# Loading a part of the gate matrix through chosen DMA engines, early in the stream

## The chip, the cores and the metric

One NeuronCore of a Trainium2 chip runs the whole kernel. The metric is the device time of one execution in microseconds (us); the time of a kernel is the median of its runs. A profile is one further execution, recorded by the hardware profiler, and its span runs from the first to the last instruction.

## The reference

A decode step for four sequences (B = 4, one token each, D = 512) mixes an attention branch and a gated feed-forward branch, with a gate g for each sequence:

```python
W = min(4096, max(256, Sk // 4))                # Sk = 16384, so W = 4096
q = (x @ wq).reshape(B, 1, 32, 128)             # 32 query heads on 8 key/value heads
scores = q . k_cache[:, :, Sk-W:, :] * 128**-0.5
a = (softmax(scores) . v_cache[:, :, Sk-W:, :]) @ wo       # wo: 4096 x 512
gate = x @ W_gate; gate = gate * (gate > 0)     # W_gate, W_up: 512 x 1792
b = (gate * (x @ W_up)) @ W_down                # W_down: 1792 x 512
g = sigmoid((x * gate_w).sum(-1))
out = g * a + (1 - g) * b
```

All inputs are bf16. The windows of the K and V caches are 64 MB, the matrices wq and wo 4 MB each, the three feed-forward matrices 1.8 MB each: 81 MB are read once for a result of 4 KB.

## The kernel before

The cache is cut into 8 sets (4 heads of one sequence each, NSET = 8). K of a set and V of a set are 4 MB each, 32 KB on every one of the 128 partitions; they pass through four such slots (NSLOT = 4). For each set VectorE transposes K in four parts (EKT, line 491), TensorE multiplies it by the query (SC), VectorE adds a mask and takes a running maximum (ESC, 527), ScalarE makes the exponentials (EXP, 619), VectorE transposes these (EPT, 542) and TensorE multiplies by V (PV). At the end come the gate and up products (GU: 16 matmuls each, 448 columns wide, 4 for each quarter q of the 512 input rows), the product with W_down (FFN), the gathering of the heads (OQ), and the product with wo (WO).

All loads are issued by SyncE's sequencer (SP), in the order of `_dma_order`: wq, x, gate_w, k 0, k 1, v 0, then k and v in turn, W_gate (`wg`), W_up, v 7, W_down, and wo in five pieces. A load into a slot waits until the one that used the slot before is done with it (`_slots`). Every engine executes its own list in order; a wait names an event that another engine or a load counts up.

A load of 128 partitions is spread over the core's 16 DMA engines, 8 partitions each. W_gate is laid out with four rows on each partition: partition p holds the rows 4p to 4p + 3 (`(p t) f -> p (t f)`), and quarter q of GU uses the rows 4p + q. x is turned to match: four small transposes (XT, line 324) take every fourth element of x, VectorE copies them to xT (EXT, 495), and ScalarE makes from the last column the gate's weights (GWB, 600).

The last piece of wo, 256 columns of 128 partitions, is not one load but three (`wo_rows`, from LOW3): of 123, 3 and 2 partitions. The page's line L256 is `load`, which issues every transfer; L320 and L324 are the helpers that issue matmuls and transposes, and L296 the one for GpSimd's masks. GpSimd (POOL) makes constants at the start, until 12.05 us, and does nothing after.

Of the kernel before, what the change touches and what calls it, by code (L numbers as in the profile page):

```python
# [5 lines left out]
FP32 = mybir.dt.float32  # L6
# [10 lines left out]
FF = 1792  # L17
# [7 lines left out]
OUTT = 2  # L25
OW = 512 // OUTT
OR = 128 // OUTT
WO_PIECES = ((0, 34), (34, 52), (52, 60), (60, 63), (63, 64))
LOW3 = (0, 123, 126, 128)

class _Plan:

# [70 lines left out]
def _alloc(nc, ctx):  # L103
    R = {}

    def sb(name, shape, dt):
        R[name] = ctx.enter_context(nc.sbuf_tensor(name, shape, dt))

    sb("slots", [128, NSLOT, 16384], BF16)
    sb("kt", [128, 4, 4096], BF16)  # L110
    sb("sc", [128, 2048], BF16)
    sb("pe", [128, 2048], BF16)
    sb("pT", [128, 2, 2048], BF16)
    sb("qblk", [128, NSET, 2, 144, 2], BF16)
    sb("xsb", [5, 512], BF16)
    sb("xT", [128, 20], BF16)
    sb("osb", [128, NSET, 512], BF16)
    sb("oq", [128, 32, 4], BF16)
    sb("identb", [128, 128], BF16)
    sb("identf", [128, 128], FP32)  # L120
    sb("ones", [128, 128], FP32)
    sb("ee", [16, 128], BF16)
    sb("e4", [16, 128], BF16)
    sb("rfold", [128, 128], FP32)
    sb("grpb", [128, 128], BF16)
    sb("own8", [128, 8], FP32)
    sb("scl", [128, 8], FP32)
    sb("maskl", [128, 128], BF16)
    sb("maskr", [128, 512], BF16)
    sb("maskf", [128, 512], BF16)  # L130
    sb("gwB", [128, 4, 128], BF16)
    sb("fold", [128, 4, 4, 64], BF16)
    sb("mx4", [128, 4], FP32)
    sb("rd32", [128, 8, 4], BF16)
    sb("negmax", [128, 2], FP32)
    sb("rowsum", [128, NSET], FP32)
    sb("recip", [128, 4, 4], FP32)
    sb("ge", [128, 2, 4], FP32)
    sb("gp", [128, 2, 4], FP32)
    sb("gg", [128, 2, 4], FP32)  # L140
    sb("hg", [128, 14, 4], BF16)
    sb("osum", [4, 512], BF16)
    R["psum"] = ctx.enter_context(nc.psum_tensor("bank", [128, 8, 512], FP32))
    return R

# [11 lines left out]


def _dma_order():
    o = [("wq",), ("x",), ("gw",), ("k", 0), ("k", 1), ("v", 0)]  # L160
    for s in range(2, NSET):
        o += [("k", s), ("v", s - 1)]
    return o + [("wg",), ("wu",), ("v", NSET - 1), ("wd",)] + [("wo", p) for p in range(len(WO_PIECES))]


def _slots():

    frees = [[] for _ in range(NSLOT)]
    at, wait = {}, {}
    turn = 0  # L170
    for it in _dma_order():
        k = it[0]
        if k in ("x", "gw") or (k == "wo" and it[1] > 0):
            continue
        if k == "wu":
            at[it] = at[("wg",)]
            wait[it] = wait[("wg",)]
            continue
        n = turn % NSLOT
        turn += 1  # L180
        at[it] = n
        wait[it] = list(frees[n])
        frees[n] = {"k": [("E", "KT", it[-1], 3)], "v": [("PV", it[-1])], "wq": [("Q", 1)], "wg": [("GU", 1)], "wd": [], "wo": []}[k]
    return at, wait


def _program(nc, plan, R, aps):
# [5 lines left out]
    xsb, xT, osb, oq = R["xsb"], R["xT"], R["osb"], R["oq"]  # L193
    identb, identf, ones = R["identb"], R["identf"], R["ones"]
    mx4, rd32, negmax, rowsum, recip = R["mx4"], R["rd32"], R["negmax"], R["rowsum"], R["recip"]
    ge, gp, gg, osum = R["ge"], R["gp"], R["gg"], R["osum"]
    consts = {"mask": R["maskf"], "grp": R["grpb"], "rfold": R["rfold"]}

    at, slot_wait = _slots()
# [39 lines left out]
        n = scf[key] - NSC  # L239
        return [("E",) + sck[n]] if n >= 0 else [("INIT",)]  # L240

    def wo_rows(p):

        return [slice(a, b) for a, b in zip(LOW3, LOW3[1:])] if p == len(WO_PIECES) - 1 else [slice(0, 128)]

    def set_of(s):
        return s % 4, s // 4
# [4 lines left out]
    def sync(e):  # L252
        E = _Eng(plan, e, "sp")

        def load(ev, ctr, dst, src, waits=()):
            E.op(lambda: e.dma_start(dst, src), ev=ev, waits=waits, ctr=ctr)  # L256

        for it in _dma_order():
            k = it[0]
            w = slot_wait.get(it, [])  # L260
            if k == "x":
                load(("X",), "d_x", xsb[0:4, :], A_x.rearrange("b o d -> (b o) d"))
            elif k == "gw":
                load(("GW",), "d_gw", xsb[4:5, :], gate_w.rearrange("(o p) -> o p", o=1))
            elif k == "wq":
                load(("WQ",), "d_wq", slot("wq"), A_wq.rearrange("(p t) f -> p (t f)", t=4), waits=w)
            elif k == "wg":
                load(("WG",), "d_wg", Wg, B_W_gate.rearrange("(p t) f -> p (t f)", t=4), waits=w)
            elif k == "wu":
                load(("WU",), "d_wu", Wu, B_W_up.rearrange("(p t) f -> p (t f)", t=4), waits=w)  # L270
            elif k == "wd":
                load(("WD",), "d_wd", Wd, B_W_down.rearrange("(p i) c -> p (i c)", i=14),
                     waits=w)
            elif k == "wo":
                lo, hi = WO_PIECES[it[1]]
                wo = A_wo.rearrange("(p i) c -> p (i c)", i=32)
                for n, r in enumerate(wo_rows(it[1])):
                    load(("WO", it[1], n), f"d_wo{it[1]}", Wo[r, OW * lo:OW * hi], wo[r, OW * lo:OW * hi], waits=w)
            else:
                b, qq = set_of(it[1])  # L280
                src = (A_k_cache if k == "k" else A_v_cache)[b, 4 * qq:4 * qq + 4, SK - WIN:SK, :]
                load((k.upper(), it[1]), f"d_{k}{it[1] % 3}", slot(*it), src.rearrange("h (r c) d -> r h (c d)", r=32),
                     waits=w)
        load(("OUT",), "d_out", out.rearrange("b o d -> (b o) d"), osum[:, :], waits=[("OSUM", 1), ("OSUM", 0)])
        E.wait([("OUT",)])

    def gpsimd(e):
# [24 lines left out]
        for g in range(8):  # L312
            v = R["fold"][:, g % 4, :, :]
            aff(v, v, [[1, 4], [-1, 64]], -64 * g, ne, 1.0, ("FOLD", g), mult=4)

    def tensor(t):
        E = _Eng(plan, t, "pe")

# [4 lines left out]
        def tp(out_, in_, idn, ev=None, waits=()):  # L323
            E.op(lambda: t.transpose(out_, in_, idn), ev=ev, waits=waits)  # L324
# [8 lines left out]
        def XT():  # L333
            bk = bankb[tr(("XT",))]
            for q in range(4):
                tp(bk[:, 6 * q:6 * q + 5], xsb[0:5, q:q + 509:4], identb[0:5, 0:5], ev=("XT",) if q == 3 else None,
                   waits=tr_free(("XT",)) + [("X",), ("GW",), ("IDB",)])

        def Z():
            for q in range(4):  # L340
# [65 lines left out]
        def GU():  # L406
            for n, (W, key) in enumerate(((Wg, "WG"), (Wu, "WU"))):
                fill = ("GU", n)
                for q in range(4):
                    for j in range(4):  # L410
                        mm(banks[scb(fill)][32 * j:32 * j + 4, 0:448], xT[:, 5 * q:5 * q + 4],
                           W[:, FF * q + 448 * j:FF * q + 448 * j + 448], q == 0, q == 3,
                           ev=fill if (q, j) == (3, 3) else None, pos=(0, 32 * j),
                           waits=sc_free(fill) + [(key,)] if (q, j) == (0, 0) else ())

        def FFN():
            for i in range(14):
# [5 lines left out]

        def WO(p):
            lo, hi = WO_PIECES[p]
            w = [("WO", p, n) for n in range(len(wo_rows(p)))] + [("E", "OQ")]
            for x in range(lo, hi):
                i, j = x // OUTT, x % OUTT
                mm(banks[ACC][OR * j:OR * j + 4, 0:OW], oq[:, i, :], Wo[:, OW * x:OW * x + OW], False, i == 31,
                   ev=("WOP", p) if x == hi - 1 else None, waits=w if x == lo else (), pos=(0, OR * j))  # L430

# [6 lines left out]
    for it in order:  # L438
# [3 lines left out]
        elif k == "CONST":  # L442
            act.append(("ECONST", it[1]))
        elif k == "XT":
            dve.append(("EXT",))
            act.append(("GWB",))
        elif k == "Z":
            act.append(("GE",))
# [33 lines left out]
    def vector(v):  # L482
        E = _Eng(plan, v, "dve")

        def INIT():
            E.op(lambda: v.memset(qblk[:, :, :, :, :].rearrange("p s h c e -> p (s h c e)"), 0.0), ev=("QZ",))  # L486
            E.op(lambda: v.memset(R["psum"][:, SCB[0]:ACC + 1, :].rearrange("p k c -> p (k c)"), 0.0), ev=("INIT",))

        def EKT(s, f):
            w = [("K", s)] + ([("SC", s - 1, f)] if s else [])  # L490
            E.op(lambda: v.transpose(kt[:, f, :].bitcast(FP32), slot("k", s)[:, 4096 * f:4096 * f + 4096].bitcast(FP32)),  # L491
                 ev=("E", "KT", s, f), waits=w)

        def EXT():
            E.op(lambda: v.tensor_copy(xT[:, :].rearrange("p (q c) -> p q c", q=4), bankb[tr(("XT",))][:, 0:24].rearrange("p (q c) -> p q c", q=4)[:, :, 0:5]), ev=("E", "XT"), waits=[("XT",)])  # L495

        def EQ(n):
            key = ("Q", n)
# [41 lines left out]

        def EPT(s):
            E.op(lambda: v.transpose(pT[:, s % 2, :], pe[:, :]), ev=("E", "PT", s),  # L542
                 waits=[("EXP", s)] + ([("PV", s - 2)] if s >= 2 else []))

        def ERS(g):
            key = ("RS", g)
# [29 lines left out]
        def FIN():  # L576
            E.op(lambda: v.tensor_copy(osum[:, OW:2 * OW], banks[ACC][OR:OR + 4, 0:OW]), ev=("OSUM", 1),  # L577
                 waits=[("WOP", len(WO_PIECES) - 1)])

        fns = dict(INIT=INIT, EKT=EKT, EXT=EXT, EQ=EQ, G=G, EQT=EQT, ESC=ESC, MAX=MAX, ESW=ESW, EPT=EPT, ERS=ERS, EOQ=EOQ, H=H,  # L580
                   EHT=EHT, FIN=FIN)
        for it in dve:
            fns[it[0]](*it[1:])
# [75 lines left out]
```

## Time and profile before

| | |
|---|---|
| median of 7 runs | 196.03 us (195.95 to 196.31) |
| the profiled execution | 196.29 us |
| its span | 195.0 us |
| TensorE matmul, busy | 121.5 us, 62% of the span |
| VectorE, busy | 124.1 us, 64% |
| ScalarE, busy | 27.5 us, 14% |
| GpSimd, busy | 9.5 us, 5% |
| DMA, read | 81.01 MB, 415 GB/s over the span |

A row such as "L491 DVE STREAM_TRANSPOSE kt<-slots ... x32 | 73.7, 2305" is a group of equal instructions: line, engine, operation, what is written from what, how many, busy microseconds in all and nanoseconds of one; after a second bar stands how long the engine idled before them and what ended that. In a table of windows each row has a stretch of time, then for each engine its busy time, and at the end the granted TensorE clock, the DMA share and the GB/s. The DMA share is the mean over the 16 DMA engines: when it falls to one half, half of them have nothing left. A packet is what a DMA engine moves at a time: here one contiguous row of a load. The chain of waits is followed back from the last instruction, at each step to what released it.

### The profile page before, as it was taken

What the parts mean: (1) busy time and instruction counts of PE and PEld (TensorE: products, weight loads), DVE (VectorE), ACT (ScalarE), POOL (GpSimd) and SP (SyncE); (2) the same over time, 40 slices, a digit from 0 to 9 for tenths busy, and PEclk for the clock granted to TensorE, in tenths of its full rate; (3) what the DMA queues carried; (4) which work ended last, traced back from release to release, by engine and by line L of the source; (5) the groups of instructions that cost most, each with busy time, mean ns of one, the idle gap of its engine ahead of it and who ended that gap; (6) DMA issues with size and microseconds to landing.
All of it is one profiled execution on the core that took longest, in us unless ns stands there. A gap on an engine that the chain in (4) does not pass through costs nothing.

```text
span 195.0 us, 1734 instructions
## 1 busy us (share of the span) xinstructions
PE 121.5 (62%) x723; PEld 50.8 (26%) x723; DVE 124.1 (64%) x153; ACT 27.5 (14%) x34; POOL 9.5 (5%) x25
## 2 busy tenths in 40 slices
PE   0209279474943864686478943894586469753974
PEld 0004123121411421242122411331142113322562
DVE  6103779999399819971998199819971998380010
ACT  2212100040130013001300130013001400420100
POOL 7830000000000000000000000000000000000000
PEclk9999957999999997899576999697999886997899
DMA  6999999999999999999999999999999999999991
GB/s 228 430 438 437 437 437 430 440 423 444 430 430 437 432 433 423 430 444 430 437 430 430 427 430 430 430 430 430 430 430 427 444 385 426 465 444 383 427 395 70
DMA packets 3616, 81.10 MB, mean 416 GB/s; under 512 B 401, under 2 KB 666, under 8 KB 794
## 3 DMA queue, kind: packets, MB, share of 16 engines
q1 hardware_dynamic: 3610, 81.01, 97.2%
q8 instruction: 5, 0.08, 0.2%
q14 instruction: 1, 0.01, 0.0%
HBM read 81.01 MB, written 0.00 MB: 415 GB/s over the span
## 4 chain that ended last, share of the span: by engine, by line
DMA 54%; DVE 29%; PE 10%; issue 5%; SPq 1%; ACT 0%
DMA slots<-in_A_k_cache_dram 38%; DVE kt L491 20%; DMA slots<-in_A_wo_dram 10%; PE bank L320 9%; DMA xsb<-in_gate_w_dram 6%; DVE sc L527 5%; DVE qblk L517 1%; PE bank L324 1%; DVE pT L542 1%; SPq L256 1%; DVE rd L531 1%; DVE negmax L537 0%; ACT gwB L600 0%; DVE osum L577 0%; DVE mx L527 0%
## 5 line engine op out<-in xcount | busy, mean ns | idle before, releaser
L491 DVE STREAM_TRANSPOSE kt<-slots 128x2048 f32<-128x2048 f32 x32 | 73.7, 2305 | 28.0 <-DMA slots<-in_A_k_cache_dram 28.0
L320 PE MATMUL bank<-kt,qblk 128*128 128x512 bf16 x256 | 73.6, 441 | 26.1 <-DVE kt L491 26.1
L320 PEld LDWEIGHTS bank<-kt,qblk 128*128 128x128 bf16 x256 | 25.6, 108 | 69.3 <-DVE kt L491 34.0
L320 PE MATMUL bank<-slots,pT 128*64 128x512 bf16 x256 | 31.8, 405 | 5.2 <-DMA slots<-in_A_v_cache_dram 5.2
L619 ACT ACTIVATE pe<-sc,negmax 128x2048 bf16<-128x2048 bf16 x8 | 16.0, 2002 | 61.9 <-DVE negmax L537 61.9
L527 DVE CUSTOM_DVE_ANT_0 sc<-bank,maskf 128x512 bf16<-128x512 f32 x32 | 21.0, 658 | 4.1 <-PE bank L320 4.1
L320 PEld LDWEIGHTS bank<-slots,pT 128*64 128x64 bf16 x256 | 15.0, 117 | 22.0 <-issue 11.8
L542 DVE STREAM_TRANSPOSE pT<-pe 128x2048 bf16<-128x2048 bf16 x8 | 18.5, 2312 | 2.2 <-ACT pe L619 2.2
L320 PE MATMUL bank<-rd,grpb 128*128 128x32 bf16 x8 | 1.6, 194 | 23.5 <-DVE rd L531 23.5
L604 ACT ACTIVATE osb<-bank 128x512 bf16<-128x512 f32 x8 | 4.8, 597 | 79.6 <-PE bank L320 79.6
L555 DVE TENSOR_TENSOR oq<-bank,recip 64x128 bf16<-64x128 f32 x2 | 0.9, 434 | 11.9 <-PE bank L320 11.9
L320 PEld LDWEIGHTS bank<-rd,grpb 128*128 128x128 bf16 x8 | 0.8, 98 | 27.0 <-DVE rd L531 27.0
L495 DVE COPY xT<-bank 128x20 bf16<-128x20 bf16 x1 | 0.2, 170 | 8.2 <-PE bank L324 8.2
L320 PE MATMUL bank<-slots,oq 128*4 128x256 bf16 x64 | 4.0, 272 | 2.0 <-DMA slots<-in_A_wo_dram 1.9
L320 PE MATMUL bank<-slots,xT 128*4 128x512 bf16 (+1 forms) x64 | 5.1, 476 | 0.0
L320 PE MATMUL bank<-maskr,maskl 128*128 128x512 bf16 x1 | 0.6, 608 | 5.9 <-POOL maskr L296 5.9
L517 DVE TENSOR_SCALAR qblk<-bank 32x64 uint32<-32x64 uint32 x16 | 2.9, 215 | 2.2 <-PE bank L324 2.1
L324 PE MATMUL bank<-identb,xsb 5*128 5x5 bf16 x4 | 0.3, 167 | 5.9 <-DMA xsb<-in_gate_w_dram 5.9
L577 DVE CAST osum<-bank 4x256 bf16<-4x256 f32 x1 | 0.4, 419 | 5.2 <-PE bank L320 5.2
L320 PEld LDWEIGHTS bank<-slots,oq 128*4 128x4 bf16 x64 | 2.5, 84 | 3.5 <-DMA slots<-in_A_wo_dram 2.9
L296 POOL TENSOR_SCALAR_AFFINE_SELECT fold<-fold 128x256 bf16<-128x256 bf16 x8 | 3.3, 417 | 1.1
L486 DVE MEMSET qblk<- 128x2304 uint32 x1 | 2.0, 1978 | 1.3 <-PEq L644 1.3
(59 smaller groups left out, 40.3 us busy)
## 6 DMA issues: line engine op xcount, KB each, us to landing
slots<-in_A_k_cache_dram SPq DMA_DIRECT2D x8, 4096.0 KB, 25.2
slots<-in_A_v_cache_dram SPq DMA_DIRECT2D x8, 4096.0 KB, 30.7
slots<-in_A_wq_dram SPq DMA_DIRECT2D x1, 4096.0 KB, 12.4
slots<-in_A_wo_dram SPq DMA_DIRECT2D x1, 2176.0 KB, 16.8
slots<-in_B_W_gate_dram SPq DMA_DIRECT2D x1, 1792.0 KB, 19.7
slots<-in_B_W_up_dram SPq DMA_DIRECT2D x1, 1792.0 KB, 23.5
slots<-in_B_W_down_dram SPq DMA_DIRECT2D x1, 1792.0 KB, 18.5
slots<-in_A_wo_dram SPq DMA_DIRECT2D x1, 1152.0 KB, 19.3
```

Of the source, the lines that this page charges most:

```text
L256: E.op(lambda: e.dma_start(dst, src), ev=ev, waits=waits, ctr=ctr)
L296: op(lambda: e.affine_select(dst, src, pattern, cmp, fill, base=base, channel_multiplier=mult), ev)
L320: E.op(lambda: t.matmul(out_, lhsT, rhs, start=start, stop=stop, tile_position=pos, skip_group_check=True), ev=ev, waits=waits)
L324: E.op(lambda: t.transpose(out_, in_, idn), ev=ev, waits=waits)
L486: E.op(lambda: v.memset(qblk[:, :, :, :, :].rearrange("p s h c e -> p (s h c e)"), 0.0), ev=("QZ",))
L491: E.op(lambda: v.transpose(kt[:, f, :].bitcast(FP32), slot("k", s)[:, 4096 * f:4096 * f + 4096].bitcast(FP32)), ev=("E", "KT", s, f), waits=w)
L517: E.op(lambda dst=dst, r=r, g=g: v.tensor_scalar(dst, src[r, g, 0:B, :, :], 0, None, op0=ALU.bitwise_or), ev=("E",) + keys[1] if (q, g) == ...
L527: E.op(lambda: v.tensor_tensor_reduce(sc[:, 512 * f:512 * f + 512], banks[scb(key)], R["maskf"][:, :], 1.0, -3.0e38, ALU.add, ALU.max, mx4 ...
L531: E.op(lambda: v.tensor_tensor(rd32[:, :, :], bc(R["own8"][:, :].unsqueeze(2), 2, 4), bc(mx4[:, :].unsqueeze(1), 1, 8), ALU.mult), ev=("MA ...
L542: E.op(lambda: v.transpose(pT[:, s % 2, :], pe[:, :]), ev=("E", "PT", s), waits=[("EXP", s)] + ([("PV", s - 2)] if s >= 2 else []))
L604: E.op(lambda: a.activation(osb[:, s, :], ob(s), ACTF.Copy), ev=("NORM", s), waits=[("PV", s)])
L619: E.op(lambda: a.activation(pe[:, :], sc[:, :], ACTF.Exp, bias=negmax[:, s % 2:s % 2 + 1], scale=SCALE, accum_out=rowsum[:, s:s + 1]), ev= ...
```

## The change

The last 896 columns of the last quarter of W_gate (the rows 4p + 3) no longer come with the main load, which so takes 12,544 bytes on each partition in place of 14,336. These 128 half rows of 1792 bytes are loaded in five transfers into a new tile, `side`, of 128 partitions with room for three half rows each (SIDE_J = 3). An entry (e, j, p, q) of SIDE is one transfer: it takes e x 4 x j rows from row p on, in e shares, and puts them on 4e partitions from partition q on, j rows on each. Together they fill 40 partitions with three rows and 8 with one; the rest of the tile is zeroed by VectorE.

The first two of these transfers are issued by SP between k 0 and k 1, the other three by GpSimd after its constants. Ahead of each of GpSimd's three stands a small "turning" load of 28, 12 or 56 rows of 128 bytes from wo into a part of the pT tile that is not yet in use; its data are never used. All five side transfers wait for the zeroing.

Because the rows lie on other partitions than in the main load, x must be laid out for them as well: five small copies on VectorE (XG) pick its elements into a zeroed part of pT, three more transposes turn them, and xT gets 15 more columns. In GU the last quarter is two matmuls from the main load and six from the side tile, so the gate product has 20 matmuls in place of 16. The first transpose into pT waits for the turning loads.

The last piece of wo is one load of 128 partitions again. The output row `osum` now shares the tile of x.

```diff
+SIDE_F, SIDE_J = 896, 3
+SIDE = ((3, 3, 0, 0), (3, 3, 36, 32), (2, 1, 120, 60), (2, 3, 72, 80), (2, 3, 96, 112))
+TURN = (0, 0, 7, 3, 14)
-LOW3 = (0, 123, 126, 128)
...
-    o = [("wq",), ("x",), ("gw",), ("k", 0), ("k", 1), ("v", 0)]
+    o = [("wq",), ("x",), ("gw",), ("k", 0), ("side", 0), ("side", 1), ("k", 1), ("v", 0)]
...
+    osum = xsb[0:4, :]
+    xg = pT[0:5, 0, 0:128 * SIDE_J].rearrange("p (j q) -> p j q", j=SIDE_J)
...
+    def side_of(n):
+        e, j, p, q = SIDE[n]
+        src = wg_all[p:p + 4 * e * j, 3 * FF + SIDE_F:4 * FF]
+        return side[q:q + 4 * e, 0:j, :], src.rearrange("(r e) f -> e r f", e=e)
+
+    def side_x(n):
+        e, j, p, q = SIDE[n]
+        src = xsb[0:5, 4 * p:4 * p + 16 * e * j].rearrange("p (r j e t) -> p j e r t", r=4, j=j, e=e, t=4)[:, :, :, :, 3]
+        return xg[:, 0:j, q:q + 4 * e].rearrange("p j (e r) -> p j e r", e=e), src
...
-                load(("WG",), "d_wg", Wg, B_W_gate.rearrange("(p t) f -> p (t f)", t=4), waits=w)
+                load(("WG",), "d_wg", Wg[:, 0:3 * FF + SIDE_F], wg_all[:, 0:3 * FF + SIDE_F], waits=w)
+            elif k == "side":
+                load(("SIDE", it[1]), f"d_side{it[1]}", *side_of(it[1]), waits=[("SZ",)])
...
-                for n, r in enumerate(wo_rows(it[1])):
-                    load(("WO", it[1], n), f"d_wo{it[1]}", Wo[r, OW * lo:OW * hi], wo[r, OW * lo:OW * hi], waits=w)
+                load(("WO", it[1]), f"d_wo{it[1]}", Wo[:, OW * lo:OW * hi], wo[:, OW * lo:OW * hi], waits=w)
...
+        rows = A_wo.rearrange("(p i) c -> p (i c)", i=4)
+        for n in range(2, len(SIDE)):
+            k, c = TURN[n], 64 * n
+            src = rows[0:4 * k, 0:64].rearrange("(r e) c -> e r c", e=k)
+            E.op(lambda k=k, c=c, src=src: e.dma_start(pT[0:4 * k, 1, c:c + 64], src), ev=("TURN", n), ctr="d_turn")
+            E.op(lambda n=n: e.dma_start(*side_of(n)), ev=("SIDE", n), waits=[("SZ",)], ctr=f"d_side{n}")
...
+            for j in range(SIDE_J):
+                tp(bk[:, 6 * (4 + j):6 * (4 + j) + 5], xg[:, j, :], identb[0:5, 0:5], ev=("XT",) if j == SIDE_J - 1 else None,
+                   waits=[("XG",)])
...
+                        of_side = n == 0 and q > 2 and 448 * j >= SIDE_F
+                        if q > 3 and not of_side:
+                            continue
+                        rhs = side[:, q - 3, x:x + 448] if of_side else W[:, FF * q + 448 * j:FF * q + 448 * j + 448]
...
+            E.op(lambda: v.memset(side[:, :, :].rearrange("p j f -> p (j f)").bitcast(FP32), 0.0), ev=("SZ",))
...
+        def XG():
+            for n in range(len(SIDE)):
+                E.op(lambda n=n: v.tensor_copy(*side_x(n)), ev=("XG",) if n == len(SIDE) - 1 else None,
+                     waits=[("X",), ("GW",), ("XGZ",)])
...
-                 waits=[("EXP", s)] + ([("PV", s - 2)] if s >= 2 else []))
+                 waits=[("EXP", s)] + ([("PV", s - 2)] if s >= 2 else [("XT",), ("TURN", len(SIDE) - 1)]))
```

## The prediction

> **What bounds the kernel now.** I read the slices of the page first, then the chain of waits, then the windows of the last microseconds, and last the trace's single DMA packets.
>
> ```profile
> DMA  6999999999999999999999999999999999999991
> q1 hardware_dynamic: 3610, 81.01, 97.2%
> q8 instruction: 5, 0.08, 0.2%
> ...
> HBM read 81.01 MB, written 0.00 MB: 415 GB/s over the span
> ```
>
> The 16 DMA engines are full in every slice between the first and the last, and no other engine is (PE 62%, DVE 64% of the span). So the bytes set the time, and the only loose ends are the start, the end, and how evenly the 16 engines finish. Nearly everything is on one queue, q1 (SP's). Beside it stand five instruction fetches, q8.
>
> ```profile
> 171.73 0.04 SPq L256
> 171.76 0.04 issue
> 171.81 0.43 SPq L256
> 172.24 0.04 issue
> 172.28 20.10 DMA slots<-in_A_wo_dram
> 192.38 0.04 issue
> 192.42 0.87 PE bank L320 x12
> 193.29 0.02 issue
> 193.32 0.42 DVE osum L577
> ```
>
> This is the tail of the chain. The last thing waited for is a landing of the Wo matrix at 192.38 us. It is the third piece: after it PE runs 12 matmuls without a break (8 of piece 2, 3 of piece 3, 1 of piece 4), so the two smaller pieces have landed by the time PE reaches them.
>
> ```profile
> 190.00:190.50 0.50, 0.32 (x6) 0.02 (x2) 0.00 (x0) 0.00 (x0) 0.00 (x0) 1.00 0.79 293
> 190.50:191.00 0.50, 0.00 (x0) 0.00 (x0) 0.00 (x0) 0.00 (x0) 0.00 (x0) 1.00 0.61 221
> 191.00:191.50 0.50, 0.36 (x8) 0.30 (x10) 0.00 (x0) 0.00 (x0) 0.00 (x0) 1.00 0.47 150
> 191.50:192.00 0.50, 0.50 (x14) 0.40 (x10) 0.00 (x0) 0.00 (x0) 0.00 (x0) 1.00 0.25 92
> 192.00:192.50 0.50, 0.36 (x8) 0.08 (x4) 0.00 (x0) 0.00 (x0) 0.00 (x0) 1.00 0.05 18
> ```
>
> The second column from the right is the DMA share. It falls in steps: some engines are done 2 us before the last. The packets say which. On one engine each packet begins as the one before ends, so packets can be strung into 16 chains. Ten chains finish piece 2 of Wo between 189.4 and 190.03 us, six between 191.0 and 191.89. Each of these six carries one instruction fetch (the five of q8, and one of 8 KB on q14). Around the first:
>
> ```
> start us   ns    bytes
> 37.718     1213  32768   (q1)
> 38.928     1042  16384   (q8, the fetch)
> 39.956     1707  32768   (q1)
> 41.659     1213  32768   (q1)
> ```
>
> The chains that load x show that engines 0 to 2 are among the early ten and engine 3 among the late six. Of engines 4 to 15 seven are early and five late; the trace does not say which.
>
> **The change part by part.** The sum is against the profiled execution, 196.29 us with a span of 195.0 (1.29 lie outside the span); the median of the runs is 196.03.
>
> *Gate load shortened.* 1792 bytes less on each partition, 8 partitions to an engine: 14,336 bytes, which is just one of its packets of before (547 at most, 539 ns at the median). Every engine: -0.54 us.
>
> *Side rows.* A row of 1792 bytes lies between the packets of 1536 (65 ns) and 4096 bytes (159 ns): 65 + 256 x 94/2560 = 74 ns. Twenty-four rows each go to engines 0, 1, 2, 12 and 13 (+1.78), four each to 7 and 8 (+0.30). [...] The trace agrees for SP: the last piece's loads of 123, 3 and 2 rows gave 3 + 3 + 2 late counts. For Pool no run shows it. Net: five engines +1.24, two -0.24, nine -0.54. [...]
>
> *Last piece of Wo.* It went as 41 + 1 + 1 packets of 512 bytes to engines 0 to 2, some 27 ns each: 1.16 us there. Now 8 packets on every engine: 0.22. It lies behind piece 2, under PE's 12 matmuls: 0 on the path, and at worst its own 0.22.
>
> *Three turning loads and three side loads on the Pool queue.* The turning loads move 7, 3 and 14 shares of four rows of 128 bytes; between 27 ns (512 bytes) and 9 ns (the 4-byte completions) I take 15: 2 x 4 x 15 = 0.12 on most engines, and 0.02 for completions. So bytes alone cost 0.14.
>
> What the trace does not show is a data packet from a second queue in the middle of the stream; the nearest row is the fetch. It took 1.04 us where 16 KB at 32,768 bytes in 1.214 us make 0.61, and the next data packet took 1.71 in place of 1.21: 0.92 over the bytes. For the six: 0.92, 0.68, 0.96, 0.95, 0.94, 0.49, mean 0.82 for each visit of another queue. [...] late engines come to -0.54 + 0.14 = -0.40. By the row, engines 0 to 13 are visited twice (14 and 15 once): 2 x 0.82 = 1.64, and the sum is +1.24. I take the row, since it is measured on this very stream; both ends are kept, the lower being zero per visit. Break-even is at 0.40/2 = 0.20 us a visit. [...]
>
> *Do the filled engines become last?* Early ones stood at 190.03 at most: + 1.24 + 1.64 + 0.14 = 193.05. The latest fetched one: 191.89 + 1.24 = 193.13. Nearly level; the latter sets the end. Without a price for visits: 191.41 against 191.49.
>
> *The start.* The side tile's zeroing is 1344 words: 1978 ns x 1344/2304 = 1.15 us, with a small one before. DVE ends its zeros near 7.0 instead of 5.5 and is idle until 13.7. SP waits for it before side 0; queued behind are k 1 and v 0, issued near 7 to 8.5 instead of 2.5 to 3.8. The stream reaches k 1 at 22.2 (chains end wq near 12.4, k 0 near 22.2), so 14 us hide it; with that cover gone it would cost 4.
>
> Five small copies on DVE now stand between x and the query (170 ns each, by the copy of xT) and three transposes (0.07 each): up to 1.06 us.
>
> ```profile
> 13.40 0.26 PE L324 MATMUL bank<-identb,xsb 5*128 5x5 bf16 x4 [5.90 <-DMA xsb<-in_gate_w_dram]
> 13.71 0.17 DVE L495 COPY xT<-bank 128x20 bf16<-128x20 bf16 x1 [8.19 <-PE bank L324]
> ```
>
> Behind them wait gwB, Z, Q and the next K load, issued at 18.28; it moves to 19.3, and its turn comes at 41.6. The chain's first long DMA piece is issued at 49.45 and lands 23.02 us later, though it needs only 9.7, so later issues have 13 us in hand too. Price if that were gone: 1.06.
>
> GU has 4 matmuls more (53 ns each, 0.21 us) at 171.6; PE next waits 5.22 us for v 7, which covers it. The wait of the first pT transpose on the last turning load: Pool is free at 12.05, six issues should end near 20, the transpose is at 41.5. SP issues two loads of Wo fewer and two side loads more. All nothing on the path. PE's 16 instructions more (7 matmuls with their weight loads, 2 waits) bring the five fetches forward a little: they come when PE has run 190, 447, 708, 969 and 1222 instructions, so a sixth would be due near 1475, where the changed program of 1475 ends, behind the last load.
>
> **The sum.** +1.24 on the engine that ends last, all of it in a stream without slack: profiled execution near 197.5, median 196.03 + 1.24 = 197.27.
>
> **The rivals.**
> *The switch costs its bytes* (the other side: faster). The late engines gain 0.40, the end moves from 192.38 to 191.98, and the five filled engines end 0.08 before them: 195.63. For it speaks that one fetch of six paid nothing on its return and another nothing on its own start, so the gap is not inherent in a switch; against it, that all six paid somewhere. It decides below 0.20 us a visit.
> *All six Pool transfers touch all engines.* 196.03 + 4.5 = 200.5. [...] Against it: completions may share a visit, which brings it down toward 198.5.
> *The rows go to other engines than meant, or a fetch falls on a filled one.* One execution moves Pool's cursor by 30 (7 + 2 + 3 + 2 + 14 + 2), so if it survives an execution the rows land two engines further back each time. On one of the late six the net is 1.24 + 0.14 in place of -0.40: even without a price for visits 191.89 + 1.38 gives 197.4, on the earliest of the six 196.5. I take 197.0. For it: the trace names only engines 0 to 3. Against it: before's runs lie within 0.36 us, so its fetches seem to fall the same way each time.
>
> **How the numbers follow.** The visits at about two per engine: 0.42, its own range 196.6 to 198.2 (0.49 to 1.2 a visit, or four cheap ones). Bytes alone: 0.40, from 195.4 to 195.9. Six visits: 0.08. Wrong engines: 0.10. Range 195.5 to 198.6: outside lie most of the six visits, a third of the bytes case's lower edge and an edge of the first, less than 0.2 together. A measurement of this kernel can tell about 0.2% (0.39 us) from no change: the bytes case, -0.40, sits on that edge, so I give faster 0.27 and same 0.13 of it; slower 0.60 is the other three.
>
> **What would show it.** Right: the first data packets of q1 after a Pool packet, between 12 and 25 us, longer than 1.21 us by 0.4 to 0.7; the K landings that follow some 1.6 us later on all engines; the gate's landing about 1.1 later. Wrong: these packets at 1.22 us, the DMA share falling more steeply after 190 us, and the last Wo landing at 192.0. Then the step that failed is the price of a visit. If the DMA slices show a gap at 22 us, the cover of k 1 was misjudged.

## The result and the profile after

The changed kernel takes 197.54 us (median of 13 runs, 196.09 to 198.37), the kernel before 196.16 us (33 runs, 195.93 to 196.45): a ratio of 1.0063, 95% interval 1.005 to 1.0076. It is slower, near the forecast of 197.3, but not by the way that the forecast took for the likeliest.

The 13 times are in two groups. Two lie at 196.09 and 196.11, with spans of 194.8 and 194.9 us; the other eleven lie between 197.28 and 198.37, with spans of 196.0 to 196.5. Before has one group (spans of 194.6 to 195.2). The profiled execution, 196.01 us with a span of 194.8, belongs to the small lower group, so its trace shows what the change costs when it goes well, and not where the median's 1.4 us come from.

The slices and the queues of the page, after:

```profile
DMA  6999999999999999999999999999999999999993
...
q1 hardware_dynamic: 3696, 80.91, 97.3%
q0 software_dynamic: 304, 0.11, 0.2%
q8 instruction: 5, 0.08, 0.2%
...
HBM read 81.02 MB, written 0.00 MB: 416 GB/s over the span
```

The DMA engines are as full as before, without a gap at 22 us. q0 is Pool's queue, new: 304 packets, which are 19 for each of the 16 engines. A packet of Pool's is not one row, as it is on q1. The packet records have 18 packets of 5376 bytes, which are three side rows (206 ns at the least), and 24 of 512 bytes, which are four turning rows (27 ns); the forecast had counted four packets of 15 ns for the latter. The end of the chain of waits, after:

```profile
168.26 4.09 PE bank L344 x35
172.43 0.43 SPq L271
172.91 19.11 DMA slots<-in_A_wo_dram
192.06 0.94 PE bank L344 x12
193.01 0.42 DVE xsb L620
```

It is the same chain. The third piece of Wo is complete near 192.0 in place of 192.38, and PE's 12 matmuls follow. The windows of the last microseconds (columns as before: the last three are the granted clock, the DMA share and GB/s):

```profile
190.00:190.50 0.50, 0.50 (x10) 0.21 (x6) 0.00 (x0) 0.00 (x0) 0.00 (x0) 1.00 0.94 364
190.50:191.00 0.50, 0.22 (x6) 0.16 (x6) 0.00 (x0) 0.00 (x0) 0.00 (x0) 1.00 0.78 308
191.00:191.50 0.50, 0.50 (x14) 0.39 (x12) 0.00 (x0) 0.00 (x0) 0.00 (x0) 1.00 0.64 247
191.50:192.00 0.50, 0.47 (x10) 0.15 (x4) 0.00 (x0) 0.00 (x0) 0.00 (x0) 1.00 0.56 189
192.00:192.50 0.50, 0.45 (x8) 0.27 (x8) 0.00 (x0) 0.00 (x0) 0.00 (x0) 1.00 0.07 21
```

The step that stood at 0.25 to 0.47 between 191 and 192 us is now at 0.56 to 0.64: eleven engines work to the end where six did. Strung into chains again (a DMA record does not name its engine; loads with particular packet sizes tell which class of engines a chain belongs to), five of the eleven carry the side rows and end their last packet of Wo's third piece between 191.24 and 191.53 us, six carry an instruction fetch and do so at 191.00 to 191.20, and none carries both. Five others are through at 189.64 to 190.19. (A landing is counted some 0.5 us after the packet: 192.01 for the last of these.)

The queue that the forecast priced at 0.82 us a visit looks like this on one of these chains (an engine without side rows, from the packet records):

```
start us   ns    bytes
22.102     1213  32768  (q1)
23.311        9      4  (q0, a completion)
23.317     1213  32768  (q1)
24.526        9     12  (q0)
24.532     1213  32768  (q1)
25.742        9     12  (q0)
25.747     1213  32768  (q1)
26.957        9     12  (q0)
26.963     1232  32768  (q1)
...
30.651       27    512  (q0, a turning row)
30.674     1225  32768  (q1)
```

On this chain a q1 packet behind a Pool packet takes 1213 to 1242 ns; on all chains of this trace they take 1213 to 1247 (one 1261), where before's packets of the same stretch take 1213 to 1220 apart from the one at the fetch. The forecast had named 1.22 us here, with a last Wo landing at 192.0, as the sign that its price of a visit was wrong. And an engine that has no share of a Pool load still handles 4-, 12- or 16-byte packets of it, of 9 to 16 ns.

The packet records also show on which chains Pool's shares lie. The data of its first four loads, 7 + 2 + 3 + 2 shares, are on 14 different chains; those of the last turning load, 14 shares, are on all chains but the two of the second side load, and the third side load is on these two again. So a load's shares fall on engines that the loads before it left out, until each has had one, and one execution moves this place on by 30 shares; it is called Pool's cursor here. SP's two side loads, with 12 rows in each share, are on the same three chains. The engines' numbers are the author's names for such chains: 0 to 2 those with SP's side rows, 7 and 8 those of Pool's first side load, 12 and 13 those of its second and third; in the other kernels they say where shares were meant to go, counted on in the same way.

The landings of one load on its 16 engines, in us, as earliest / median / latest:

```
                  before                      after
wq            12.40 / 12.74 / 13.21     12.61 / 12.72 / 12.97
v 0           41.61 / 41.90 / 43.32     42.14 / 42.51 / 44.17
v 6           158.14 / 158.65 / 160.13  158.78 / 160.28 / 160.73
wg            162.43 / 162.93 / 164.40  162.54 / 164.04 / 164.49
wo, 3rd piece 189.99 / 190.49 / 192.38  190.14 / 191.61 / 192.01
```

At v 0 the earliest landing is 0.53 later, but this is not all Pool's: 0.21 of it stands at wq already, before Pool's first packet (they lie between 16.3 and 38.7 us). The chains tell it better. Worked out from the packet records, a chain's time in us between the ends of its shares of four loads; an engine is called plain where it has neither side rows nor a fetch in the first stretch:

```
                                       before              after
end of wq to end of k 2, plain         38.72 to 38.83      39.07 to 39.18
  with 24 side rows                                        40.63 to 41.00
end of k 2 to end of v 6, no fetch     106.79 to 106.86    106.82 to 106.91
  with a fetch of 16 KB                108.38 to 108.41    108.38 to 108.40
the gate                               4.29 to 4.31        3.76 to 3.77
```

So Pool's six loads cost a plain engine 0.35 to 0.4 us (0.39 by the means), and the gate's cut gives 0.53 back. Twenty-four side rows cost a chain 1.5 to 1.9 us, and a fetch of 16 KB makes its chain some 1.55 us late. In this trace the filled engines end last, at 191.53, where before the latest fetched chain ended at 191.89; that is about the 0.37 by which the landing is earlier. The lower group's times, 196.09 and 196.11, lie inside before's spread around 196.16, so no gain is shown.

### The profile page after: what moved, and what is told of

It is laid out like the page before. It is cut to its first block, busy times and chain, and to the rows that moved or that the text cites. A ratio compares the mean times of both kernels' runs of the same rounds, so it can differ in the third digit from the quotient of the medians.

```text
span 194.8 us, 1765 instructions
## 1 busy us (share of the span) xinstructions
PE 122.1 (63%) x730; PEld 51.3 (26%) x730; DVE 126.2 (65%) x160; ACT 27.5 (14%) x34; POOL 13.2 (7%) x31
## 4 chain that ended last, share of the span: by engine, by line
DMA 54%; DVE 29%; PE 11%; issue 4%; SPq 0%; ACT 0%
DMA slots<-in_A_k_cache_dram 38%; DVE kt L529 20%; DMA slots<-in_A_wo_dram 10%; PE bank L344 9%; DMA xsb<-in_A_x_dram 6%; DVE sc L570 5%; DVE qblk L560 1%; PE bank L348 1%; DVE pT L585 1%; DVE rd L574 1%; SPq L271 0%; ACT gwB L643 0%; DVE pT L534 0%; DVE negmax L580 0%; DVE xsb L620 0%
## 5 line engine op out<-in xcount | busy, mean ns | idle before, releaser
L344 PE MATMUL bank<-slots,xT 128*4 128x512 bf16 (+1 forms) x62 | 5.6, 488 | 0.0
L534 DVE COPY pT<-xsb 5x36 bf16<-5x36 bf16 (+2 forms) x5 | 0.6, 178 | 6.0 <-DMA xsb<-in_A_x_dram 6.0
L580 DVE TENSOR_REDUCE negmax<-bank 128x1 f32<-128x32 f32 x8 | 1.5, 192 | 2.0 <-PE bank L344 2.0
```

Of the source, the lines that this page charges most:

```text
L344: E.op(lambda: t.matmul(out_, lhsT, rhs, start=start, stop=stop, tile_position=pos, skip_group_check=True), ev=ev, waits=waits)
L580: E.op(lambda: v.tensor_reduce(negmax[:, s % 2:s % 2 + 1], banks[tr(key)][:, 0:32], AXIS.X, ALU.min), ev=("E",) + key, waits=[key])
```

## The experiments

The question is where the upper group's 1.3 us come from. The meeting theory: in those executions an instruction fetch falls on an engine that carries side rows; that chain is then late by both. The queue theory: Pool's queue, in its visits, takes that time in some executions. The fill theory: the filled engines end last by themselves, without a fetch.

**The cursor made neutral.** A turning load of two shares more, Pool's seventh load, so that one execution moves Pool's cursor by 32 shares in place of 30.

```diff
-TURN = (0, 0, 7, 3, 14)
+TURN = (0, 0, 7, 3, 14, 2)
...
```

> The changed kernel with one more turning load of two shares at the end of Pool's list, so that Pool's cursor advances by 32 in each execution in place of 30. Theory (the cursor survives an execution, so the side rows land two DMA engines further back each time, mostly on engines that are late already): every run like the changed kernel's profiled one, 195.9 to 196.3 us, none above 196.6. Rival (each visit of Pool's queue costs a DMA engine some 0.8 us): no better than the change, 197.3 to 199. Rival (the spread is noise of the Pool queue): spread of over 1 us stays, median near 197.5.

Measured: 197.40 us (6 runs, 196.27 to 197.65), ratio 1.0056 (1.0038 to 1.0075), two with spans of 195.0 and four with 196.1 to 196.4. The same two groups: an advance of 30 that survives the execution is not, alone, what makes them.

**Pool's pairs on other engines.**

```diff
-TURN = (0, 0, 7, 3, 14)
+TURN = (0, 0, 5, 3, 14, 4)
...
```

> As neutral, 32 in all, but the turning loads are of 5, 3, 14 and 4 shares, so that the side rows meant for engines 12 and 13 are carried by 10 and 11, and those of 7 and 8 by 5 and 6: the place they would have in the second execution if the cursor survives. Theory: one steady time, 197.2 to 197.8 if engine 10 or 11 carries an instruction fetch (1.8 us on top of a late engine, less the 0.4 that late engines gained), 196.0 to 196.3 if neither does. Rivals: as the change, 197.5 with a spread of over 1 us.

Measured: 198.26 us (4 runs, 197.6 to 199.16), ratio 1.011 (1.0088 to 1.0133), profiled span 196.9. In its trace the fetch at 40.6 us falls on a chain with side rows of Pool. That chain ends its last packet of Wo's third piece at 193.69, the next one at 193.12. The rest of the loss lies earlier and was not expected: between 20 and 45 us 134 of the 32 KB packets are longer than 1.27 us (1 in the trace of the change, a fetch's neighbour), 1.1 us on each engine in all, and v 0 lands at 43.58 at the median.

**No Pool.** The 56 rows that Pool carried go in one SP transfer of 14 shares, 4 rows to an engine; Pool's six loads are gone.

```diff
-SIDE = ((3, 3, 0, 0), (3, 3, 36, 32), (2, 1, 120, 60), (2, 3, 72, 80), (2, 3, 96, 112))
-TURN = (0, 0, 7, 3, 14)
+SIDE = ((3, 3, 0, 0), (3, 3, 36, 32), (14, 1, 72, 64))
...
```

> The side rows without Pool: the first two transfers as in the change (72 rows on engines 0 to 2), the other 56 rows in one transfer from SP, in 14 shares of four rows on engines 0 to 13; no turning loads. Late engines lose 0.54 and get 0.30 back (14 and 15: nothing back), engines 0 to 2 get 28 rows (2.1 us) less 0.54. By the packets of before the end moves by 0.24 to 0.3: 195.75 to 195.95, steady. If the change's loss came from the shortened gate load, the copies at the start or the one-piece end of Wo, this loses too: above 196.6.

Measured: 196.52 us (9 runs, 196.47 to 197.53), ratio 1.003 (1.0018 to 1.0042). No span is over 195.6, so the upper group is gone. The gain that was expected did not come either. The kernel's own loss of 0.35 us has a place: between 20 and 26 us, where the wide transfer passes, 35 packets of 32 KB are longer than 1.27 us, 0.4 us on each engine.

**Small Pool loads alone.** Before, with twelve turning loads on Pool and nothing else.

```diff
+TURN = (7, 2, 3, 2, 14, 4) * 2
...
+        for n, k in enumerate(TURN):
+            src = rows[0:4 * k, 0:64].rearrange("(r e) c -> e r c", e=k)
+            E.op(lambda ...: e.dma_start(pT[0:4 * k, 1, 64 * n:64 * n + 64], src), ev=("TURN", n), ctr="d_turn")
...
```

> The kernel before with twelve turning loads from Pool added (128-byte rows; 7, 2, 3, 2, 14, 4 shares, twice, 64 in all), nothing else changed. If a visit costs what its packets take (0.02 us each, two on every engine for each load): +0.5 us, 196.5 to 196.8. If each load costs a DMA engine what an instruction fetch did over its bytes (0.82 us): +9.8 us where every engine is visited, +4.5 where only the shares are.

Measured: 198.05 us (4 runs, 197.83 to 198.29), ratio 1.0097 (1.0084 to 1.011). v 0 lands 1.09 us later at the median engine (42.99 against 41.90). 384 packets are 24 on an engine: 0.045 us each, 0.09 for a load. The end of its chain of waits:

```profile
174.70 19.69 DMA slots<-in_A_wo_dram
194.43 0.87 PE bank L325 x12
```

The end moves by 2.0 us. The chain that carries the fetch at 40.3 us took 42.53 us from the end of wq to the end of k 2, where before's with the fetch of the same stretch took 40.29: another 1.1 beyond the 1.09, and it ends last. So twelve Pool loads cost real time, more than the 0.5 expected from their packets alone, but less on the median engine than the forecast's two visits (1.64).

**The change once more, twice, for its trace.** No edit.

> The changed kernel as it is, looked at once more for its packets. Theory (TensorE's instruction fetches fall on other DMA engines from execution to execution, five of the engines 4 to 15, and one execution is slow when one of them falls on 12 or 13, which the side rows have filled): if the time is near 196.1 no fetch stands on a chain with side rows from Pool; if it is near 197.5 at least one does, and that chain lands last, some 1.4 us behind the others. Rival (Pool's packets cost more in some executions): in a slow one all 16 chains are later by 0.7 us or more at the landing of v 0 than in a fast one, whatever engine has the fetches. Rival (the cursor survives): the side rows stand on other chains than engines 12 and 13.

> A further execution of the changed kernel, with the same expectations as the look before it: near 196.1 without a fetch on a chain that Pool's side rows filled, near 197.5 with one; by the rivals, all chains later at v 0, or the rows on other engines.

Measured: 196.40 us (span 195.1) and 196.67 us (span 194.7). Both executions were of the lower kind again by their spans, with no fetch on a chain with Pool's side rows. This agrees with the meeting theory but does not show the other case.

**Pool kept, its rows spread.** The wide transfer of the no-Pool kernel, but issued by Pool, without turning loads.

```diff
-SIDE = ((3, 3, 0, 0), (3, 3, 36, 32), (2, 1, 120, 60), (2, 3, 72, 80), (2, 3, 96, 112))
+SIDE = ((3, 3, 0, 0), (3, 3, 36, 32), (14, 1, 72, 64))
...
-            E.op(lambda k=k, c=c, src=src: e.dma_start(pT[0:4 * k, 1, c:c + 64], src), ev=("TURN", n), ctr="d_turn")
```

> The side rows of Pool in one transfer of 14 shares, four rows on each of 14 engines, in place of three transfers that fill 12 and 13; no turning loads; SP's two transfers to engines 0 to 2 stay. Theory (a filled engine 12 or 13 that gets a fetch is what makes an execution slow): no engine is filled where fetches fall, so no second group of times 1.3 us above the first; median 195.9 to 196.4, spread under 0.7. Rival (Pool's queue makes some executions slow): the second group near 197.4 stays. By the price of my prediction (0.82 a visit): one visit, -0.54 + 0.30 + 0.82, 196.6.

Measured: 196.36 us (21 runs, 196.1 to 198.03), ratio 1.0016 (1.0006 to 1.0026), all spans between 194.9 and 195.6. No upper group; one time, 198.03, is high outside its span (195.6). Engines 0 to 2 are filled here as in the change, so the fill theory does not hold for them. The group needs Pool's 24 rows on a pair of engines, or the five Pool loads more that this kernel has not.

**Pool's pair alone.** SP's two side loads are left out (72 rows of the gate's last columns count as zero), Pool's six loads are as in the change.

```diff
-    o = [("wq",), ("x",), ("gw",), ("k", 0), ("side", 0), ("side", 1), ("k", 1), ("v", 0)]
+    o = [("wq",), ("x",), ("gw",), ("k", 0), ("k", 1), ("v", 0)]
...
-                            w = [("SIDE", g) for g in range(len(SIDE))]
+                            w = [("SIDE", g) for g in range(2, len(SIDE))]
```

> This kernel leaves SP's two side loads out (72 rows of the last gate columns are counted as zero), keeps the shortened gate, and keeps Pool's three turning loads and three side loads as in the change: 24 rows on each of engines 12 and 13, 4 on each of 7 and 8. Theory 'fetch on a Pool pair' (in most executions one of PE's five instruction fetches falls on engine 12 or 13, which are filled): two groups of times stay, a small one near 196.1 and most runs at 197.3 to 197.7, since the chain that sets the end there carries 24 rows and a fetch and does not need engines 0 to 2. Theory 'the five filled engines are all too late': with 0 to 2 unfilled the group near 197.4 would shrink but not go. Theory 'Pool's pair moves to other engines in each execution': two groups as well.

Measured: 197.75 us (6 runs, 197.33 to 198.77), ratio 1.0086 (1.0068 to 1.0105), all six with spans of 196.1 to 196.5. The small group near 196.1 that was expected does not show in these six. With engines 0 to 2 unfilled the upper group is whole, so it does not need them. The profiled execution is one of the six, so the upper kind can be looked at here. Its windows of the end:

```profile
191.00:191.50 0.50, 0.50 (x15) 0.40 (x12) 0.00 (x0) 0.00 (x0) 0.00 (x0) 1.00 0.41 160
191.50:192.00 0.50, 0.50 (x14) 0.42 (x10) 0.00 (x0) 0.00 (x0) 0.00 (x0) 1.00 0.21 74
192.00:192.50 0.50, 0.50 (x14) 0.31 (x12) 0.00 (x0) 0.00 (x0) 0.00 (x0) 1.00 0.15 59
192.50:193.00 0.50, 0.50 (x14) 0.41 (x10) 0.00 (x0) 0.00 (x0) 0.00 (x0) 1.00 0.11 44
193.00:193.50 0.50, 0.43 (x10) 0.12 (x7) 0.00 (x0) 0.00 (x0) 0.00 (x0) 1.00 0.13 49
193.50:194.00 0.50, 0.50 (x10) 0.26 (x11) 0.00 (x0) 0.00 (x0) 0.00 (x0) 1.00 0.05 13
```

From 192 to 193.5 us the DMA share stays near 0.13. That is two engines of sixteen, which work alone for 1.5 us. The end of the chain of waits of the same execution:

```profile
173.79 19.64 DMA slots<-in_A_wo_dram
193.47 0.95 PE bank L344 x12
```

The third piece of Wo is complete at 193.43, 1.05 us later than before (192.38). Strung into chains, the two late ones are the two that carry Pool's 24 side rows, and these two also carry the fetches at 149.2 and 183.5 us. Their last packets of the piece end at 192.97 and 193.00; every other chain is through by 191.37. The 32 KB packets of this trace are otherwise hardly disturbed (six are longer than 1.27 us, five of them at fetches). That is the meeting, seen. Its size fits the change too: there the filled chains ended at 191.24 to 191.53, and a fetch of 1.55 us on one of them would make 192.8 to 193.1, which is 1.3 to 1.6 after the end that was traced (an estimate from these two rows). The upper group's spans are 1.2 to 1.7 us above the traced one.

**Pool's pair on engines 0 and 1.** The same, with 7 shares in the second turning load, which is meant to put the pair there.

```diff
-TURN = (0, 0, 7, 3, 14)
+TURN = (0, 0, 7, 7, 14)
```

> The kernel of the same set that leaves SP's two side loads out, with the second turning load of 7 shares in place of 3, which puts the two side loads of 24 rows in all on engines 0 and 1 in place of 12 and 13 if Pool's cursor starts at 0; the number of Pool's transfers is the same. Theory 'fetch on a Pool pair': no fetch was seen on engines 0 to 2 in any trace, so no second group: all runs within 195.8 to 196.4. Theory 'Pool's pair moves to other engines in each execution' (the cursor is advanced by 34 here, by 30 in the change): two groups stay, with runs at 197.3 to 197.7.

Measured: 197.28 us (7 runs, 196.64 to 198.93), ratio 1.007 (1.0043 to 1.0098). Two runs have spans near 195.4, five have 196.0 to 196.7. So the expectation of the meeting theory in the form "engines 0 to 2 are never hit" failed. In the profiled execution (196.77) no fetch falls on the pair, yet v 0 lands at 43.33 at the median: between 20 and 45 us 118 packets of 32 KB are longer than 1.27 us, 1.1 us on each engine, as with the pairs at 5, 6, 10 and 11. What differs in the five long executions, a fetch on the pair or something else, is not known: none of them was traced.

**One part alone: the last piece of Wo in one load.** Before, with

```diff
-LOW3 = (0, 123, 126, 128)
+LOW3 = (0, 128)
```

> The kernel before with one part of the change alone: the last piece of Wo is one load of 128 rows over 16 engines in place of three loads of 123, 3 and 2 rows over engines 0 to 2. By the prediction it costs nothing on the path: 196.1 to 196.3, ratio 0.999 to 1.001. Rival: on the six late engines it adds its own 0.22 us behind piece 2 and shows in the end: up to 196.4.

Measured: 196.08 us (13 runs, 195.92 to 196.49), ratio 0.9998 (0.999 to 1.0006). Nothing, as predicted.

**SP alone, half the columns, engines 0 to 2 alone.**

```diff
-SIDE_F, SIDE_J = 896, 3
-SIDE = ((3, 3, 0, 0), (3, 3, 36, 32), (14, 1, 72, 64))
+SIDE_F, SIDE_J = 1344, 3
+SIDE = ((3, 3, 0, 0), (3, 3, 36, 32), (3, 3, 72, 64), (3, 1, 108, 96), (2, 1, 120, 112))
...
```

(against the kernel without Pool)

> A way that leaves Pool and the wide transfer out: only 448 columns are cut from the gate (0.27 us less on every engine), and their 128 rows of 896 bytes go by five SP loads onto engines 0 to 2 alone, 40 to 44 rows each, at some 45 ns a row by interpolation between the packets of 512 and 1536 bytes (27 and 65 ns): +1.9 there, net +1.65 on chains that end at 190.03 at most, so 191.7, level with the late ones at 191.89 - 0.27. If the fill of engines 0 to 2 costs its bytes and nothing else: 195.9, ratio 0.9987. If five small loads from SP disturb the stream like the load of 14 shares did (0.4 us an engine): 196.4 or more.

Measured: 196.77 us (9 runs, 196.48 to 197.68), ratio 1.0043 (1.0028 to 1.0059). Filling engines 0 to 2 goes with a disturbance of all the others (17 packets of 32 KB of 1.3 us or more between 20 and 26 us, about 0.5 us an engine), and the filled chains end level with the fetched ones (third piece of Wo 192.1 at the median, 192.62 at the latest). It beats neither the kernel before nor the one without Pool.

**The change with rows of half the size.** All loads, engines and queues as in the change; only the size differs.

```diff
-SIDE_F, SIDE_J = 896, 3
+SIDE_F, SIDE_J = 1344, 3
```

> The change with one size altered: 448 columns are cut and carried in place of 896, so each side row is 896 bytes and costs some 43 ns (the kernel that filled engines 0 to 2 alone: 40 to 44 rows took 1.7 to 1.9 us there) in place of 74 to 80, and the gate's cut is 0.27 us in place of 0.54. Loads, engines and queues are the same. Theory 'a fetch on a filled engine sets the end': its net is 24 x 0.043 - 0.27 = +0.76 in place of +1.24 to +1.4, so the group near 197.5 moves down to 196.8 to 197.0, and the group near 196.1 stays between 196.0 and 196.4; median 196.9. Theory 'Pool's queue costs that much whatever it carries': the group near 197.5 stays or rises by the 0.27 that the gate no longer gives.

Measured: 196.64 us (22 runs, 196.02 to 197.35), ratio 1.0025 (1.0014 to 1.0036). The spans are no longer parted by a gap: thirteen lie at 194.8 to 195.3 and nine at 195.5 to 196.1. Taken as the upper group, the nine have a median span of 195.8 where the change's upper group has 196.2, so the distance to before's (194.9) falls from 1.3 to 0.9. The rows' net cost was to fall from 1.24 to 0.76, so the expected ratio was 0.61; measured are 0.9/1.3 = 0.69. A fixed price of Pool's queue would have left 1.3 or more, and the longest span here is 1.2 above before's. So the upper group's cost goes with the bytes of the side rows. One thing was not expected: nine of 22 executions are of the upper kind, where it was eleven of 13 in the change, which is why the median is 196.64 and not 196.9. Why a smaller row should meet a fetch less often is open.

None of the twelve beats the kernel before by more than its measurement is uncertain.

## Why the prediction was right, and where it was not

The time was forecast at 197.3 and is 197.54. The number came out by luck: the forecast added 1.64 us for visits that cost 0.4, and left at a chance of 0.10 the meeting of a fetch and a filled engine, which brings most executions to about the same time. The step that failed is **the price of a visit of Pool's queue**.

- *Gate load shortened, -0.54.* Right: 4.29 us became 3.76 on every engine.
- *Side rows, +1.78 on five engines.* Nearly right in size: a filled chain took 1.5 to 1.9 us more than a plain one; one of SP's took 1.95 us for its 24 rows (22.20 to 24.16, with two completions and 13 Pool packets in it). In the traces of the change the rows are on five chains without a fetch, as was meant.
- *Last piece of Wo, nothing on the path.* Right: 0.9998 for the kernel with this part alone.
- *A visit at 0.82 us, two on most engines: 1.64.* Wrong. A q1 packet behind a Pool packet takes 0 to 34 ns more (once 48), and all of Pool's six loads together cost a plain engine 0.35 to 0.4 us. The row taken for the price, the fetch, was not near: its packets are 16 KB, Pool's are 4 to 512 bytes on most engines. Over two visits it makes 0.2 us a visit, at the break-even of 0.20 that the forecast gave. With 0.39 in place of 1.64 and 0.14 the forecast's own sum is -0.15, or 195.9, which is no change that could be told apart. The lower group, at 196.1, is near it.
- *The rival that all six Pool transfers touch all engines, with 4.5.* That was the author's estimate: six visits of every engine at 0.82 (4.9), with the late engines' -0.40. The trace shows the visits: q0 has 19 packets for each engine, chains without a share have completions of 4 bytes too, and the landing records have 16 counts for each of Pool's six loads, of 2 to 14 shares, where they have 4 for each of SP's side loads, of three. But they cost 0.4 and not 4.9. The packets above show the order, one of Pool's before each of SP's, and the runs the price, 0.02 us a packet in the change (0.39 over 19) and 0.045 with twelve small loads. The other end, "bytes alone" with 0.14, was below that.
- *Filled engines nearly level with the fetched ones.* Right in the profiled execution: 191.53 at the latest against 191.20, where 191.41 against 191.49 had been worked out without a price for visits.
- *The rival "the rows go to other engines than meant, or a fetch falls on a filled one".* It was given a chance of 0.10 and 196.5 to 197.4. By what the runs show it is the case of most executions: the upper group begins at 197.28 and its middle is 197.54. The traces of Pool's pair alone and of the pairs on other engines show its second half, a fetch on a filled engine; without Pool, and with Pool's rows spread, the group is gone; and the half-size rows show that its cost goes with the rows' bytes. The chance was too low because before's runs lie so close together that the fetches seemed to fall the same way each time. But before has no filled engine that a fetch could hurt more than another: its end is that of the latest fetched chain (191.89, where the latest without a fetch ended at 190.03), whichever that is. So its narrow spread could not tell where the fetches fall.
- *The start.* The covers held. SP's k 1 and v 0 were issued at 8.89 and 9.51, later than the 7 to 8.5 worked out, and found 13 us of cover. The zeroing took 1.18 us where 1.15 had been worked out, the five copies 0.60 together where 0.85 had been. The next K load was issued at 18.80 (before 18.28). The timeline of after:

```profile
5.99 1.18 DVE L525 MEMSET side<- 128x1344 f32 x1 [0.27 <-issue]
7.20 1.65 SPq L271 DMA_DIRECT2D side<-in_B_W_gate_dram  x2
8.89 0.58 SPq L271 DMA_DIRECT2D slots<-in_A_k_cache_dram  x1
9.51 0.60 SPq L271 DMA_DIRECT2D slots<-in_A_v_cache_dram  x1
...
13.16 0.60 DVE L534 COPY pT<-xsb 5x36 bf16<-5x36 bf16 x5 [6.00 <-DMA xsb<-in_A_x_dram]
```

- *A sixth instruction fetch, behind the last load.* Right where it is seen: of the change's three traces the last has it, at 195.9 us, after the span of 194.7, and 1.97 us of that execution lie outside its span in place of 1.2 to 1.3. The two highest runs of the change, 198.37 and 198.06, have 2.37 and 1.86 outside their spans. That the same fetch is the cause there was not traced.

Open stays what moves from one execution to the next, so that a filled engine and a fetch seem to meet in eleven executions of thirteen: the fetches, or Pool's cursor and with it the pair. No fetch lay on the pair in the three traces of the change, two did in that of Pool's pair alone and one in that of the pairs on other engines, so which chains they share does change between kernels. The records don't name a DMA engine, so the traces don't settle where the cursor starts. All four profiled executions of the change and of the neutral cursor were of the lower kind, while two of the change's thirteen timed ones were, which would suit a cursor that starts at the same place whenever a kernel is loaded (a guess, not shown); that the neutral cursor left the groups in place speaks against it. An execution of the change itself of the upper kind was not traced, so for the change the meeting is argued from the other kernels and not seen.

## What to carry to other kernels

In a stream that keeps all DMA engines full, giving some engines more bytes evens out only what is late the same way in each execution. Lateness that is not bound to an engine (here an instruction fetch of 16 KB, which makes its engine 1.55 us late from there on) can fall on the filled engines, and then both add up (the two chains with both ended at 193.0 with Pool's pair alone, every other by 191.37); so a profile in which the fill fits is one draw, and the spread of the timed runs and their spans must be read beside it. Before pricing a second queue by a row of another kind, ask whether its packets are of that row's size (a fetch of 16 KB took 0.82 us over its bytes, Pool's packets of 4 to 512 bytes some 0.02 each).

## What was not expected of the hardware

- Which engines Pool's 24-row pairs are on changed how much the whole stream was disturbed. Between 20 and 45 us, 1 or 2 packets of 32 KB were longer than 1.27 us with the pair meant for 12 and 13 (the change, twice more the change, Pool's pair alone), 134 with pairs meant for 5, 6, 10 and 11, and 118 with the pair meant for 0 and 1, each by some 0.15 us, 1.1 us on each engine in all. Why is open.
- A small transfer on Pool's queue cost the median DMA engine some 0.09 us, though it moves 4 to 512 bytes there (1.09 us for twelve).
- While a transfer of 56 rows of 1792 bytes over 14 engines passed on SP's queue, 35 packets of 32 KB took 1.27 to 1.56 us in place of 1.21.
